# Weaving attention and channel work by hand on TensorE: a four-batch attention and ResMLP kernel

## The chip, the cores and the metric

The kernel runs on one core of a Trainium2 chip. The metric is the device time of one execution in microseconds (us); lower is better. The profile is one traced execution. Its engines are PE (TensorE, matmuls), PEld (its weight loads), DVE (VectorE), ACT (ScalarE), POOL (GpSimd) and SP (SyncE, which here only issues transfers).

## The reference

Shapes: batch 4, 8 heads, 768 positions, head width 64; then a block of width 512 with a hidden width of 2048.

```python
# P: 8 x 8 per head, five rounds of exp and row/column normalising of sort_net
k_sorted = einsum('bhij,bhjcd->bhicd', P, k_blocks)      # mixes blocks of 96 positions
v_sorted = einsum('bhij,bhjcd->bhicd', P, v_blocks)
scores = q_block @ k_sorted_block.T / 8                   # inside each block only
x = softmax(scores) @ v_sorted_block                      # -> (b, 768, 512)
u = x + lam * einsum('ts,bsd->btd', w_tok, alpha1 * x + beta1)
out = u + lam * (relu((alpha2 * u + beta2) @ w_ch1) @ w_ch2)
```

## The kernel before

Each batch does the same work on TensorE. I use the kernel's names: **v** and **k** mix the blocks of values and keys; **sc** (scores) and **x** (value products) are the attention; **tok** is the position mix, which needs all of x; **h** and **ch** are the two channel layers, in two halves (hf) of three tiles each. The work of one batch's attention runs beside the channel layers of the batch before. A small class wraps each engine; where its `fixed` is set, instructions keep the order in which the program names them, and elsewhere a scheduler orders them when the program is built.

```python
    class Engine:
        ...
                ins = getattr(self.eng, name)(*args, **kwargs)
                if self.fixed:
                    tc.keep_in_program_order(ins)

    def load_q(b):            # queries of batches 2, 3: six loads by GpSimd, one buffer
        ...
        qn = att.tile([128, NT, H, D], F16, name="qn", tag="qn", bufs=1)
        for kt in range(NT):
            pool.dma_start(qn[:, kt, :, :], q[b].rearrange("h (p kt) d -> kt p h d", kt=NT)[kt])

    def cross_q(b):           # ... and six transposes, issued by SyncE
        with tc.issue_after(regroup[b - 1].ins):
            for kt in range(NT):
                nc.sync.dma_start_transpose(
                    qT_of[b][:, :, kt, :], qn_of[b][:, kt, :, :].rearrange("p h d -> p (h d)")
                )

    def mix_v(b, banks=2, ...):
        ...                    # matmuls into PSUM, copies to vA, then through memory and back:
        nc.sync.dma_start(vscr[b, ...], vA[...])                       # x2
        regroup[b] = nc.sync.dma_start(Vs[b % NV][...], vscr[b]...)    # x2

    def emit_attention(b):
        ...
        prev = [emit_scores(b, 0, g) for g in range(2)]
        for h4 in range(1, H4):
            cur = [emit_scores(b, h4, g) for g in range(2)]
            emit_pv(b, h4 - 1, prev, x128, xs)       # value products; VectorE evicts them
            prev = cur
            if h4 == H4 - 1:
                gather(0, 384)                       # three small copies into x
        emit_pv(b, H4 - 1, prev, x128, xs)
        gather(384, C)

    def moe_ch(b, hf, kks=range(3)):
        for kk in kks:
            kt = 3 * hf + kk
            ...
            ost = att.tile([128, C], FT, name="ost", tag="ost", bufs=2)
            ...                # 16 matmuls into cps
                dve.tensor_tensor(cps[:], cps[:], lamB[:, lo:hi], ALU.mult)
                dve.tensor_tensor(ost[:, lo:hi], cps[:], u_of[b][kt][:, lo:hi], ALU.add)
                nc.sync.dma_start(out[b, kt * 96:(kt + 1) * 96, lo:hi], ost[0:96, lo:hi])
                ...            # and one more store of 32 rows

    # the main loop (TensorE, ScalarE, VectorE not fixed from here on)
    for b in range(1, B):
        if b > 1:
            if b > 2:
                cross_q(b)
            mixing_matrices(b)
            mix_v(b)
            ...
            mix_k(b)
        emit_attention(b)
        if b == 1:
            moe_ch(0, 0, (2,))
        else:
            moe_h(b - 1, 0)
            moe_ch(b - 1, 0)
        moe_h(b - 1, 1)
        moe_a(b)                                    # tok, and the transposes of u
        moe_ch(b - 1, 1)
        if b == 1:
            load_q(2)
            cross_q(2)
```

The softmax here doesn't subtract the row's maximum and nothing guards it: scores larger than these inputs give would overflow.

Of the kernel before, what the change touches and what calls it, by code (L numbers as in the profile page):

```python
# [7 lines left out]
FT = mybir.dt.float32  # L8
F16 = mybir.dt.float16
# [7 lines left out]
def kernel(  # L17
# [24 lines left out]
    BLK = S // NB  # L42
# [212 lines left out]
    def load_weights():  # L255
        for g in range(4):
            pool.dma_start(W1p[:, :, g * 512:(g + 1) * 512], w1v[:, :, g * 512:(g + 1) * 512])
        load_raw(1, 1)
        for g in range(4):
            pool.dma_start(W2p[:, g * 4:(g + 1) * 4, :], w2v[:, g * 4:(g + 1) * 4, :])  # L260

# [65 lines left out]
    def mix_v(b, banks=2, groups=range(6), copies=(act.copy, dve.tensor_copy, act.copy)):  # L327
        raw = raw_of[(b, 1)]
        lhsT = bigV[b][:].rearrange("p g i -> p (g i)")
        if b not in vA_of:  # L330
            vA_of[b] = att.tile([128, HB, D], F16, name="vA", tag="vA", bufs=1)
        vA = vA_of[b]
        for n in groups[::banks]:
            vps = (psb if banks == 1 else psa)([128, banks, 512], FT, "v_ps")
            for nn in range(banks):
                pe.matmul(vps[:, nn, :], lhsT, raw[:, (n + nn) * 512:(n + nn + 1) * 512], start=True, stop=True)
            copies[n // banks % len(copies)](
                vA[:, n * 8:(n + banks) * 8, :].rearrange("p t d -> p (t d)"), vps[:].rearrange("p n x -> p (n x)")
            )
        if groups[-1] < 5:  # L340
            return
        for th in range(2):
            nc.sync.dma_start(
                vscr[b, :, :, th * HB:(th + 1) * HB, :].rearrange("h i t d -> (h i) t d"),
                vA[th * 64:(th + 1) * 64, :, :],
            )
        for par in range(2):
            regroup[b] = nc.sync.dma_start(
                Vs[b % NV][par * HB:(par + 1) * HB, :, 0:D],
                vscr[b].rearrange("h i (tt par) d -> par tt (h i) d", par=2)[par],  # L350
            )

    def mix_k(b, share=(4, 0, 4), gs=range(3)):
        raw = raw_of[(b, 0)]
        rhs = bigP[b][:].rearrange("p g i -> p (g i)")
        if b not in kT_of:
            kT_of[b] = att.tile([128, H4 * NB, BLK], F16, name="kT", tag="kT", bufs=2)
        kv_ = kT_of[b][:].rearrange("p c (par th tp) -> p th c par tp", th=2, par=2)
        for g in gs:
            kps = psa([128, 8, 128], FT, "k_ps")  # L360
            for tp in range(8):
                t0 = (8 * g + tp) * 128
                pe.matmul(kps[:, tp, :], raw[:, t0:t0 + 128], rhs, start=True, stop=True)
            for par in range(2):
                for h2 in range(2):
                    src = kps[par * 64:(par + 1) * 64, :, h2 * 64:(h2 + 1) * 64].rearrange(
                        "p n (th c) -> p th c n", th=2
                    )
                    dst = kv_[h2 * 64:(h2 + 1) * 64, :, :, par, 8 * g:8 * g + 8]
                    if 2 * par + h2 < share[g]:  # L370
                        dve.tensor_copy(dst, src)
                    else:
                        act.copy(dst, src)
# [15 lines left out]

    def mix_k0(h4):  # L390
        if 0 not in kT_of:
            kT_of[0] = att.tile([128, H4 * NB, BLK], F16, name="kT", tag="kT", bufs=2)
        mix_heads(0, h4, kT_of[0][:, h4 * NB:(h4 + 1) * NB, :], (act.copy, dve.tensor_copy))

    vT0 = []
# [13 lines left out]

    x_of = {}  # L410

    def emit_scores(b, h4, g, spins=0):
        kT = kT_of[b]
        qT = qT_of[b]
        blocks = ((0, 1, 2, 6), (3, 4, 5, 7))[g] if b == 0 else range(4 * g, 4 * g + 4)
        sps = psa([128, 2, 4, 128], FT, "sc_ps")
        spin(sps[:, 0, :, :].rearrange("p i x -> p (i x)"), spins)
        for ii, i in enumerate(blocks):
            for h2 in range(2):
                rows = slice(h2 * 64, (h2 + 1) * 64)  # L420
                pe.matmul(
                    sps[0:BLK, h2, ii, 0:BLK], kT[rows, h4 * NB + i, :], qT[rows, h4, :, i * 16:(i + 1) * 16],
                    start=True, stop=True,
                )
        et = att.tile([BLK, 2, 4, BLK], F16, name="et", tag="et", bufs=4)
        act.activation(
            et[:].rearrange("p a i (r kt) -> p (a i) r kt", kt=NT),
            sps[0:BLK].rearrange("p a i x -> p (a i) x")[:, :, 0:BLK].rearrange("p n (kt r) -> p n r kt", kt=NT),
            AF.Exp, scale=scale,
        )  # L430
        return et
# [49 lines left out]
            xps[:, :, :, 0:D], recip[:].unsqueeze(3).to_broadcast([128, 2, 3, D]), ALU.mult,  # L481
        )

    def emit_attention(b):
        x128 = moep.tile([128, NT, C], F16, name="x128", tag="x128", bufs=2)
        xs = moep.tile([BLK, 2, C], F16, name="xs", tag="xs", bufs=1)
        x_of[b] = x128

        def gather(lo, hi):
            for a in range(3):  # L490
                dve.tensor_copy(x128[96:128, a:a + 4:3, lo:hi], xs[32 * a:32 * a + 32, :, lo:hi])

        prev = [emit_scores(b, 0, g) for g in range(2)]
        for h4 in range(1, H4):
            cur = [emit_scores(b, h4, g) for g in range(2)]
            emit_pv(b, h4 - 1, prev, x128, xs)
            prev = cur
            if h4 == H4 - 1:
                gather(0, 384)
        emit_pv(b, H4 - 1, prev, x128, xs)  # L500
        gather(384, C)


    w_tokT = const([128, NT, S], F16, "w_tokT")
    rs = const([128, NT], FT, "rs")
# [131 lines left out]

    def moe_h(b, hf, which=range(HT)):
        if (b, hf) not in hT_of:
            hTa = moep.tile([128, 12, 384], BF, name="hTa", tag="big", bufs=1)  # L640
            hTb = moep.tile([128, HT - 12, 384], BF, name="hTb", tag="hTb", bufs=1)
            hT_of[(b, hf)] = [hTa[:, m, :] if m < 12 else hTb[:, m - 12, :] for m in range(HT)]
        for m in which:
            hps = psb([128, 384], FT, "h_ps")
            for ci in range(CT):
                pe.matmul(
                    hps[:], W1p[:, ci, m * 128:(m + 1) * 128], a2T_of[b][hf][:, ci, :],
                    start=(ci == 0), stop=(ci == CT - 1),
                )
            act.activation(hT_of[(b, hf)][m], hps[:], AF.Relu)  # L650

    def moe_ch(b, hf, kks=range(3)):
        hT = hT_of[(b, hf)]
        for kk in kks:
# [3 lines left out]
            for lo, hi in ((0, 384), (384, C)) if last else ((0, C),):  # L658
                cps = psb([128, hi - lo], FT, "ch_ps")
                for m in range(HT):  # L660
                    pe.matmul(
                        cps[:], hT[m][:, kk * 128:(kk + 1) * 128], W2p[:, m, lo:hi],
                        start=(m == 0), stop=(m == HT - 1),
                    )
                dve.tensor_tensor(cps[:], cps[:], lamB[:, lo:hi], ALU.mult)
                dve.tensor_tensor(ost[:, lo:hi], cps[:], u_of[b][kt][:, lo:hi], ALU.add)
                nc.sync.dma_start(out[b, kt * 96:(kt + 1) * 96, lo:hi], ost[0:96, lo:hi])
                (nc.scalar if last else nc.sync).dma_start(
                    out[b, TAIL + kt * 32:TAIL + (kt + 1) * 32, lo:hi], ost[96:128, lo:hi]
                )  # L670


    ets = {}
# [51 lines left out]
    moe_row(range(2, NT))  # L725
    for kt in range(2, NT):
        moe_add(0, kt)
    load_raw(1, 0)
    load_q(1)
    for kt in range(2):  # L730
        dve.scalar_tensor_tensor(
            u_of[0][kt][:], b1lB[:], rs[:, kt:kt + 1], x_of[0][:, kt, :], op0=ALU.mult, op1=ALU.add
# [12 lines left out]
    stack = ExitStack()  # L745
    for eng in order:
        stack.enter_context(tc.issue_after(eng.ins))
    moe_h(0, 0, range(5))
    for n in range(6):
        moe_h(0, 0, range(5 + n, 6 + n))  # L750
        mix_v(1, 1, range(n, n + 1), (dve.tensor_copy,))
    pool.tensor_copy(gate[:], Vs[1][0:1, 0, 0:2])
    load_raw(2, 1)
    load_raw(2, 0)
    pool.fixed = False
    moe_h(0, 0, range(11, HT))
    moe_turn(0, 1)
    stack.close()
    pe.fixed = True
    for kk in range(2):  # L760
        moe_ch(0, 0, (kk,))
        mix_k(1, gs=((0, 1), (2,))[kk])
        for h4 in range(2 * kk, 2 * kk + 2):
            turn_q(1, h4, dve.tensor_copy)
    pe.fixed = False
    for b in range(1, B):
        if b > 1:
            if b > 2:
                cross_q(b)
            mixing_matrices(b)  # L770
            mix_v(b)
            if b == 2:
                opened = pool.tensor_copy(gate[:], Vs[0][0:1, 0, 0:2])
                with tc.issue_after(opened.ins):
                    load_q(3)
                    load_raw(3, 1)
                    load_raw(3, 0)
            mix_k(b)
        emit_attention(b)
        if b == 1:  # L780
            moe_ch(0, 0, (2,))
        else:
            moe_h(b - 1, 0)
            moe_ch(b - 1, 0)
        moe_h(b - 1, 1)
        moe_a(b)
        moe_ch(b - 1, 1)
        if b == 1:
            load_q(2)
            cross_q(2)  # L790
    for hf in range(2):
        moe_h(B - 1, hf)
        moe_ch(B - 1, hf)


# [28 lines left out]
```

## Time and profile before

| | before |
|---|---|
| median of 3 runs | 268.52 us (268.40 to 269.82) |
| profiled span | 266.8 us, full TensorE clock |
| TensorE busy | 257.6 us, 97% |
| batches 1, 2 and 3 (my cuts) | 60.8, 58.8, 58.8 us |

The lines themselves are in the prediction. "Busy" of TensorE is modelled and overlaps, so the prediction works with the distance from one matmul's start to the next.

### The profile page before, as it was taken

What the parts mean: (1) busy time and instruction counts of PE and PEld (TensorE: products, weight loads), DVE (VectorE), ACT (ScalarE), POOL (GpSimd) and SP (SyncE); (2) the same over time, 40 slices, a digit from 0 to 9 for tenths busy, and PEclk for the clock granted to TensorE, in tenths of its full rate; (3) what the DMA queues carried; (4) which work ended last, traced back from release to release, by engine and by line L of the source; (5) the groups of instructions that cost most, each with busy time, mean ns of one, the idle gap of its engine ahead of it and who ended that gap; (6) DMA issues with size and microseconds to landing.
All of it is one profiled execution on the core that took longest, in us unless ns stands there. A gap on an engine that the chain in (4) does not pass through costs nothing.

```text
span 266.8 us, 5149 instructions
## 1 busy us (share of the span) xinstructions
PE 257.6 (97%) x2049; PEld 141.6 (53%) x2059; DVE 154.8 (58%) x333; ACT 125.8 (47%) x232; POOL 92.5 (35%) x100
## 2 busy tenths in 40 slices
PE   7799999999999999999999999999999999999993
PEld 2467745565565444554565444554565445545542
DVE  5878788629567966722585966704675962042033
ACT  3376757643585312980375404970474305504600
POOL 8524689203575615007917225002409000000000
PEclk9999999999999999999999999999999999999999
DMA  6999999999999544499996342494200432012012
GB/s 83 174 208 251 207 210 207 211 216 112 211 157 155 113 84 117 114 82 89 202 211 136 61 100 80 118 98 62 80 2 2 81 76 79 2 39 79 2 39 79
DMA packets 62423, 30.88 MB, mean 116 GB/s; under 512 B 48888, under 2 KB 58112, under 8 KB 62400
## 3 DMA queue, kind: packets, MB, share of 16 engines
q0 software_dynamic: 23024, 15.60, 39.4%
q1 hardware_dynamic: 39280, 14.89, 32.6%
q8 instruction: 16, 0.26, 0.4%
q14 instruction: 7, 0.06, 0.1%
q10 hardware_dynamic: 96, 0.07, 0.1%
HBM read 32.78 MB, written 8.65 MB: 155 GB/s over the span
## 4 chain that ended last, share of the span: by engine, by line
PE 89%; ACT 4%; DVE 4%; issue 1%; DMA 1%; DVEq 0%; ACTq 0%
PE ch_ps L65 31%; PE h_ps L65 30%; PE tok_ps L65 12%; PE x_ps L65 5%; PE sc_ps L65 4%; ACT kT L65 2%; PE v_ps L65 2%; PE k_ps L65 1%; PE q_ps L65 1%; ACT et L65 1%; DVE csum L65 1%; DVE P L65 1%; PE m_ps L65 1%; DVE rsum L65 1%; DMA P<-in_sort_net_dram 1%
## 5 line engine op out<-in xcount | busy, mean ns | idle before, releaser
L65 PE MATMUL h_ps<-a2T,W1p 128*128 128x384 bf16 x512 | 93.4, 326 | 0.1
L65 ACT ACTIVATE hTa<-h_ps 128x384 bf16<-128x384 f32 x96 | 45.9, 492 | 68.1 <-PE h_ps L65 67.0
L65 PE MATMUL ch_ps<-W2p,hTa 128*128 128x512 bf16 (+2 forms) x290 | 65.9, 370 | 0.5
L65 PEld LDWEIGHTS <-W1p 128*128 128x128 bf16 x512 | 47.5, 98 | 30.3 <-issue 0.9
L65 DVE TENSOR_TENSOR ch_ps<-ch_ps,lamB 128x512 f32<-128x512 f32 (+2 forms) x25 | 16.9, 676 | 63.2 <-PE ch_ps L65 60.5
L65 POOL TENSOR_SCALAR u<-b1lB,rs 128x512 f32<-128x512 f32 x18 | 28.8, 1610 | 64.1 <-DVE ost L65 59.3
L65 PEld LDWEIGHTS <-hTa 128*128 128x128 bf16 x300 | 28.7, 98 | 32.4
L65 PE MATMUL tok_ps<-x,w_tokT 128*128 128x512 f16 x144 | 32.1, 379 | 0.0
L65 POOL TENSOR_TENSOR u<-x,u 128x512 f32<-128x512 f16 x22 | 25.3, 1181 | 18.1 <-DVE x L65 17.3
L65 ACT ACTIVATE et<-sc_ps 96x768 f16<-96x768 f32 x32 | 24.9, 807 | 11.7 <-PE sc_ps L65 11.7
L65 ACT CAST u<-u 128x512 f16<-128x512 f32 x24 | 14.8, 618 | 24.8 <-DVE u L65 24.8
L65 PE MATMUL ch_ps<-W2p,hTb 128*128 128x512 bf16 (+2 forms) x100 | 25.0, 371 | 0.0
L65 PEld LDWEIGHTS <-w_tokT 128*128 128x128 f16 x180 | 14.8, 97 | 16.1
L65 DVE TENSOR_TENSOR tok_ps<-tok_ps,a1lB 128x512 f32<-128x512 f32 x24 | 16.5, 692 | 7.3 <-PE tok_ps L65 7.3
L65 DVE CAST kT<-k_ps 64x512 f16<-64x512 f32 x24 | 16.5, 688 | 3.4 <-PE k_ps L65 3.0
L65 DVE TENSOR_TENSOR x<-x_ps,recip 96x512 f16<-96x512 f32 (+2 forms) x32 | 17.6, 554 | 0.9
L65 DVE TENSOR_TENSOR u<-tok_ps,u 128x512 f32<-128x512 f32 x24 | 16.4, 688 | 1.7
L65 ACT ACTIVATE hTb<-h_ps 128x384 bf16<-128x384 f32 x32 | 15.3, 497 | 3.8 <-PE h_ps L65 3.4
L65 DVE TENSOR_TENSOR ost<-ch_ps,u 128x512 f32<-128x512 f32 (+2 forms) x25 | 16.6, 665 | 0.6
L65 POOL DMA_DIRECT2D qn<-in_q_dram x18 | 15.5, 875 | 4.2 <-PE q_ps L65 3.4
L65 PEld LDWEIGHTS <-hTb 128*128 128x128 bf16 x100 | 9.6, 98 | 10.9
L65 PEld LDWEIGHTS <-et 96*128 96x128 f16 (+2 forms) x288 | 12.4, 99 | 4.6 <-issue 1.2
(95 smaller groups left out, 214.7 us busy)
## 6 DMA issues: line engine op xcount, KB each, us to landing
out_dram<-ost SPq DMA_DIRECT2D x23, 192.0 KB, 2.2
raw<-in_v_dram POOLq DMA_DIRECT2D x8, 384.0 KB, 8.9
raw<-in_k_dram POOLq DMA_DIRECT2D x8, 384.0 KB, 10.9
vscr<-vA SPq DMA_DIRECT2D x6, 384.0 KB, 4.4
Vs<-vscr SPq DMA_DIRECT2D x6, 384.0 KB, 7.7
W1p<-in_moe_w_ch_dram POOLq DMA_DIRECT2D x4, 512.0 KB, 10.1
W2p<-in_moe_w_ch_dram POOLq DMA_DIRECT2D x4, 512.0 KB, 17.9
qn<-in_q_dram POOLq DMA_DIRECT2D x12, 128.0 KB, 5.8
```

Source lines behind the costliest of these rows:

```text
L65: ins = getattr(self.eng, name)(*args, **kwargs)
```

## The change

Its intent is to spend channel matmuls as filler: whenever the attention would wait for an eviction, a counted number of h or ch matmuls stands in between. Both score groups of a head pair are issued together. Batch 1's key mixes and query transposes move into the first channel layer. W2 is loaded later, batch 1's keys and queries earlier. In batch 1's attention, five output tiles (ch(0,0) and two tiles of ch(0,1)) are now computed where the h work of the second half stood.

```diff
+        load_raw(1, 0)            # in load_weights, ahead of W2
+        load_q(1)
+    def load_w2():                # called later, where these two loads were
...
-            kT_of[b] = att.tile([...], name="kT", tag="kT", bufs=2)
+            kT_of[b] = att.tile([...], name="kT", tag="kT", bufs=1)
...
+    def emit_pair(b, h4):
+        pair = [psa([128, 2, 4, 128], FT, "sc_ps") for _ in range(2)]
+        for g in range(2):
+            score(b, h4, range(4 * g, 4 * g + 4), pair[g])
+        return [emit_exp(ps) for ps in pair]
...
+        yield 0, lambda: scores(0)          # attention_steps: (us of filler ahead, step)
+        yield 2.4, lambda: scores(1)
+        yield first, lambda: values(0)
+        yield 2.2, lambda: scores(2)
+        yield 2.4, lambda: values(1)
+        yield 2.2, lambda: scores(3)
+        yield 2.4, lambda: values(2)
+        yield 2.4, lambda: values(3)        # values(2), values(3) also gather into x
...
-            hTa = moep.tile([128, 12, 384], BF, name="hTa", tag="big", bufs=1)
-            hTb = moep.tile([128, HT - 12, 384], BF, name="hTb", tag="hTb", bufs=1)
+            hT = moep.tile([128, HT, 384], BF, name="hT", tag=("big", "hT1")[hf], bufs=1)
...                                          # moe_h yields 0.65 per tile, moe_ch 0.216 per matmul
+    for n in range(3):                      # inside the first channel layer
+        mix_k(1, gs=(n,))
+        run(moe_h(0, 0, range(10 + 2 * n, 11 + 2 * n)))
+        turn_q(1, n, dve.tensor_copy)
+        run(moe_h(0, 0, range(11 + 2 * n, min(12 + 2 * n, HT))))
+    turn_q(1, 3, dve.tensor_copy)
...
     for b in range(1, B):
+        if b == 1:
+            fill = chain(moe_h(0, 1), moe_ch(0, 0), moe_ch(0, 1, (0, 1)))
+            steps = [(0.6, lambda: mixing_matrices(2)), (0.6, lambda: mixing_matrices(3)), (0.8, lambda: None)]
+        else:
+            fill = chain(moe_h(b - 1, 0), moe_ch(b - 1, 0), moe_h(b - 1, 1), moe_ch(b - 1, 1, (0,)))
+            steps = [...]                   # mixes of v and k, with 1.8 to 3.0 us between
+        weave(fill, steps + list(attention_steps(b, 5.6 if b == 1 else 5.3)))
+        run(fill)
         moe_a(b)
-        moe_ch(b - 1, 1)
+        run(moe_ch(b - 1, 1, (2,) if b == 1 else (1, 2)))
         if b == 1:
             load_q(2)
             cross_q(2)
```

More of the change, by code (lines that the diff above doesn't have):

```diff
@@ L332, in mix_v @@
         vA = vA_of[b]
-        for n in groups[::banks]:
+        for n in range(groups[0], groups[-1] + 1, banks):
             vps = (psb if banks == 1 else psa)([128, banks, 512], FT, "v_ps")
@@ L356, in mix_k @@
         if b not in kT_of:
-            kT_of[b] = att.tile([128, H4 * NB, BLK], F16, name="kT", tag="kT", bufs=2)
+            kT_of[b] = att.tile([128, H4 * NB, BLK], F16, name="kT", tag="kT", bufs=1)
         kv_ = kT_of[b][:].rearrange("p c (par th tp) -> p th c par tp", th=2, par=2)
@@ L391, in mix_k0 @@
         if 0 not in kT_of:
-            kT_of[0] = att.tile([128, H4 * NB, BLK], F16, name="kT", tag="kT", bufs=2)
+            kT_of[0] = att.tile([128, H4 * NB, BLK], F16, name="kT", tag="kT", bufs=1)
         mix_heads(0, h4, kT_of[0][:, h4 * NB:(h4 + 1) * NB, :], (act.copy, dve.tensor_copy))
@@ L410, with score @@
     x_of = {}
-    def emit_scores(b, h4, g, spins=0):
-        kT = kT_of[b]
-        qT = qT_of[b]
-        blocks = ((0, 1, 2, 6), (3, 4, 5, 7))[g] if b == 0 else range(4 * g, 4 * g + 4)
-        sps = psa([128, 2, 4, 128], FT, "sc_ps")
-        spin(sps[:, 0, :, :].rearrange("p i x -> p (i x)"), spins)
+    def score(b, h4, blocks, sps):
         for ii, i in enumerate(blocks):
@@ L421, in emit_scores, with emit_exp @@
                 pe.matmul(
-                    sps[0:BLK, h2, ii, 0:BLK], kT[rows, h4 * NB + i, :], qT[rows, h4, :, i * 16:(i + 1) * 16],
-                    start=True, stop=True,
-                )
+                    sps[0:BLK, h2, ii, 0:BLK], kT_of[b][rows, h4 * NB + i, :],
+                    qT_of[b][rows, h4, :, i * 16:(i + 1) * 16], start=True, stop=True,
+                )
+    def emit_pair(b, h4):
[3 more added lines that the diff above has]
+        return [emit_exp(ps) for ps in pair]
+    def emit_scores(b, h4, g, spins=0):
+        sps = psa([128, 2, 4, 128], FT, "sc_ps")
+        spin(sps[:, 0, :, :].rearrange("p i x -> p (i x)"), spins)
+        score(b, h4, ((0, 1, 2, 6), (3, 4, 5, 7))[g], sps)
+        return emit_exp(sps)
+    def emit_exp(sps):
         et = att.tile([BLK, 2, 4, BLK], F16, name="et", tag="et", bufs=4)
@@ L482, in pv_tiles, with attention_steps @@
         )
-    def emit_attention(b):
+    def attention_steps(b, first):
         x128 = moep.tile([128, NT, C], F16, name="x128", tag="x128", bufs=2)
@@ L487, in emit_attention, with scores, values, weave @@
         x_of[b] = x128
-        def gather(lo, hi):
-            for a in range(3):
-                dve.tensor_copy(x128[96:128, a:a + 4:3, lo:hi], xs[32 * a:32 * a + 32, :, lo:hi])
-        prev = [emit_scores(b, 0, g) for g in range(2)]
-        for h4 in range(1, H4):
-            cur = [emit_scores(b, h4, g) for g in range(2)]
-            emit_pv(b, h4 - 1, prev, x128, xs)
-            prev = cur
-            if h4 == H4 - 1:
-                gather(0, 384)
-        emit_pv(b, H4 - 1, prev, x128, xs)
-        gather(384, C)
+        ets = {}
+        def scores(h4):
+            ets[h4] = emit_pair(b, h4)
+        def values(h4):
+            emit_pv(b, h4, ets[h4], x128, xs)
+            if h4 > 1:
+                lo, hi = ((0, 384), (384, C))[h4 - 2]
+                for a in range(3):
+                    dve.tensor_copy(x128[96:128, a:a + 4:3, lo:hi], xs[32 * a:32 * a + 32, :, lo:hi])
+        yield 0, lambda: scores(0)
[6 more added lines that the diff above has]
+        yield 2.4, lambda: values(3)
+    def weave(fill, steps):
+        for gap, step in steps:
+            filled = 0
+            while filled < gap:
+                took = next(fill, None)
+                if took is None:
+                    break
+                filled += took
+            step()
     w_tokT = const([128, NT, S], F16, "w_tokT")
@@ L639, in moe_h @@
         if (b, hf) not in hT_of:
-            hTa = moep.tile([128, 12, 384], BF, name="hTa", tag="big", bufs=1)
-            hTb = moep.tile([128, HT - 12, 384], BF, name="hTb", tag="hTb", bufs=1)
-            hT_of[(b, hf)] = [hTa[:, m, :] if m < 12 else hTb[:, m - 12, :] for m in range(HT)]
+            hT = moep.tile([128, HT, 384], BF, name="hT", tag=("big", "hT1")[hf], bufs=1)
+            hT_of[(b, hf)] = [hT[:, m, :] for m in range(HT)]
         for m in which:
@@ L650, in moe_h @@
             act.activation(hT_of[(b, hf)][m], hps[:], AF.Relu)
+            yield 0.65
     def moe_ch(b, hf, kks=range(3)):
@@ L664, in moe_ch @@
                     )
+                    if m < HT - 1:
+                        yield 0.216
                 dve.tensor_tensor(cps[:], cps[:], lamB[:, lo:hi], ALU.mult)
@@ L670, in moe_ch, with run @@
                 )
+                yield 0.216
+    def run(units):
+        for _ in units:
+            pass
     ets = {}
@@ L727 @@
         moe_add(0, kt)
-    load_raw(1, 0)
-    load_q(1)
+    load_w2()
     for kt in range(2):
@@ L747 @@
         stack.enter_context(tc.issue_after(eng.ins))
-    moe_h(0, 0, range(5))
+    pe.fixed = True
+    run(moe_h(0, 0, range(3)))
     for n in range(6):
-        moe_h(0, 0, range(5 + n, 6 + n))
+        run(moe_h(0, 0, range(3 + n, 4 + n)))
         mix_v(1, 1, range(n, n + 1), (dve.tensor_copy,))
@@ L755 @@
     pool.fixed = False
-    moe_h(0, 0, range(11, HT))
+    run(moe_h(0, 0, range(9, 10)))
     moe_turn(0, 1)
+    for n in range(3):
[4 more added lines that the diff above has]
+    turn_q(1, 3, dve.tensor_copy)
     stack.close()
     pe.fixed = True
-    for kk in range(2):
-        moe_ch(0, 0, (kk,))
-        mix_k(1, gs=((0, 1), (2,))[kk])
-        for h4 in range(2 * kk, 2 * kk + 2):
-            turn_q(1, h4, dve.tensor_copy)
@@ L765, with chain, mixes @@
-    pe.fixed = False
+    def chain(*parts):
+        for part in parts:
+            yield from part
+    def mixes(b, n):
+        return lambda: mix_v(b, 2, range(2 * n, 2 * n + 2), ((act.copy, dve.tensor_copy, act.copy)[n],) * 3)
     for b in range(1, B):
-        if b > 1:
+        if b == 1:
+            fill = chain(moe_h(0, 1), moe_ch(0, 0), moe_ch(0, 1, (0, 1)))
+            steps = [(0.6, lambda: mixing_matrices(2)), (0.6, lambda: mixing_matrices(3)), (0.8, lambda: None)]
+        else:
@@ L768 @@
             if b > 2:
                 cross_q(b)
-            mixing_matrices(b)
-            mix_v(b)
-            if b == 2:
-                opened = pool.tensor_copy(gate[:], Vs[0][0:1, 0, 0:2])
-                with tc.issue_after(opened.ins):
-                    load_q(3)
-                    load_raw(3, 1)
-                    load_raw(3, 0)
-            mix_k(b)
-        emit_attention(b)
-        if b == 1:
-            moe_ch(0, 0, (2,))
-        else:
-            moe_h(b - 1, 0)
-            moe_ch(b - 1, 0)
@@ L785, with later @@
-        moe_h(b - 1, 1)
+            fill = chain(moe_h(b - 1, 0), moe_ch(b - 1, 0), moe_h(b - 1, 1), moe_ch(b - 1, 1, (0,)))
+            steps = [
+                (0.0, mixes(b, 0)), (0.0, mixes(b, 1)), (1.8, mixes(b, 2)),
+                (1.8, lambda: mix_k(b, gs=(0,))), (1.8, lambda: mix_k(b, gs=(1,))),
+                (2.4, lambda: mix_k(b, gs=(2,))), (3.0, lambda: None),
+            ]
+            if b == 2:
+                def later():
+                    opened = pool.tensor_copy(gate[:], Vs[0][0:1, 0, 0:2])
+                    with tc.issue_after(opened.ins):
+                        load_q(3)
+                        load_raw(3, 1)
+                        load_raw(3, 0)
+                steps.insert(3, (0.0, later))
@@ L791 @@
     for hf in range(2):
-        moe_h(B - 1, hf)
-        moe_ch(B - 1, hf)
+        run(moe_h(B - 1, hf))
+        run(moe_ch(B - 1, hf))
 _INS = ['q', 'k', 'v', 'sort_net', 'moe_alpha1', 'moe_beta1', 'moe_w_tok', 'moe_alpha2', 'moe_beta2', 'moe_w_ch1', 'moe_w_ch2', 'moe_lam']
```

## The prediction

> **What bounds the kernel now.** I read the page's busy table and its chain first, then a table of stretches, one per batch, then the TensorE timeline inside one stretch. The page:
>
> ```profile
> PE 257.6 (97%) x2049; PEld 141.6 (53%) x2059; DVE 154.8 (58%) x333; ACT 125.8 (47%) x232; POOL 92.5 (35%) x100
> ...
> PE 89%; ACT 4%; DVE 4%; issue 1%; DMA 1%; DVEq 0%; ACTq 0%
> ```
>
> TensorE is busy 97% of the span and is 89% of the chain that ended last. A busy figure of modelled, overlapping ends doesn't say how much is lost, so I cut the span at the points where one batch hands over to the next (my cuts: the first h_ps matmul of batch 0 at 42.7, the mixing-matrix matmul of batch 2 at 103.5, that of batch 3 at 162.3, and the end of batch 3's attention round at 221.1):
>
> ```profile
> 42.70:103.50 60.80, 60.55 (x476) 33.19 (x478) 42.24 (x82) 29.37 (x55) 26.19 (x28) 1.00 1.07 156
> 103.50:162.30 58.80, 58.49 (x419) 30.78 (x420) 35.10 (x71) 28.24 (x52) 24.58 (x24) 1.00 0.84 121
> 162.30:221.10 58.80, 58.49 (x420) 30.90 (x422) 35.10 (x71) 28.25 (x52) 14.19 (x11) 1.00 0.42 71
> 221.10:262.50 41.40, 41.30 (x238) 22.71 (x238) 8.94 (x14) 15.71 (x32) 0.00 (x0) 1.00 0.14 40
> ```
>
> The columns are the stretch, its length, then busy us of PE, PEld, DVE, ACT, POOL, the clock, DMA. The clock is full throughout. The first three stretches are what the change rewrites: 178.4 us. The last one and everything before 42.7 keep their order of work.
>
> Next, what a matmul really takes: the distance of one start to the next, from the timeline. In long runs this is 162 ns for h_ps, 216 for ch_ps, tok_ps and v_ps, 56 for k_ps and uT_ps. These are full-array matmuls (128 rows), and they follow each other without loss. The score matmuls, 64 rows each, do not:
>
> ```profile
> 115.39 0.33 PE L65 MATMUL h_ps<-a2T,W1p 128*128 128x384 bf16 x1
> 115.65 0.56 PE L65 MATMUL sc_ps<-qT,kT 64*96 64x96 f16 x15
> 116.14 0.66 PE L65 MATMUL h_ps<-a2T,W1p 128*128 128x384 bf16 x3
> 116.92 0.38 PE L65 MATMUL sc_ps<-qT,kT 64*96 64x96 f16 x8
> 117.23 0.50 PE L65 MATMUL h_ps<-a2T,W1p 128*128 128x384 bf16 x2
> 117.66 0.38 PE L65 MATMUL sc_ps<-qT,kT 64*96 64x96 f16 x8
> ```
>
> The single h at 115.39 is followed at 115.65: 0.256 us instead of 0.162, so 0.093 us on the way in. Eight scores then hold TensorE 0.31 us (116.92 to 117.23), but fifteen only 0.49 (115.65 to 116.14). So seven more scores cost 0.18, or 25 ns each, and a fixed part of about 0.11 is the way out. **A lone group of 8 costs 0.093 + 0.311 = 0.404; a group of 16 would cost about 0.093 + 0.512 = 0.605.**
>
> **What the Trainium skill says.** "TensorEngine Tiling (Array Packing)", Key Properties: "Changing tiling mode (not just tile) drains the TensorE". The trace agrees: loss appears only where 64-row scores or 64-column q transposes meet full-array work (q group, way in 0.093), not at h to v or h to k. "TensorE: Matmul & The Clock Gate", Part 3, says that matmuls keep strict order and only weight loads are pulled ahead; so a matmul that waits holds all behind it, and a fixed order moves where the waits fall. "SBUF — State Buffer", on the pair of ports that VectorE and GpSimd share, calls it an exclusive lock. The trace is consistent: the last of three small copies into x takes up to 1.11 us (shortest 0.22) while GpSimd's first add runs.
>
> **The change, part by part.**
>
> *Scores in pairs.* Both groups of a head pair are issued back to back: four blocks of 16 in place of eight of 8 per batch. 8 x 0.404 = 3.23 becomes 4 x 0.605 = 2.42: minus 0.81 per batch, three batches, all on the path.
>
> *Batches 2 and 3: the stretch summed.* Full-array work: h 128 x 0.1624 = 20.79, ch 96 x 0.216 = 20.73, tok 36 x 0.216 = 7.77, v 6 x 0.216 = 1.30, k 24 x 0.056 = 1.35; together 51.94. Before: plus scores 3.23, value products 8 blocks x 0.257 = 2.06, the mixing matmul and its two switches 0.23: 57.46. Measured 58.8, so 1.3 us are true waits. I find them in the unmerged timeline: two waits of 0.17 before k_ps, 0.22 before an h, 0.18 before v_ps, 0.19 before a score, two of 0.12 before value products. All are cases of an operand or PSUM pair not yet evicted. The weave puts 1.8 to 3.0 us of h or ch between them. I check one: k_ps g0 needs four VectorE copies of 0.69 = 2.8 us; its PSUM is wanted again after two fills, 1.95 + 2.6 us. Good. After: 51.94 + 2.42 + 2.05 = 56.41 without waits, a gain of 2.4.
>
> *The wait that the weave adds.* The fill of batch 2 is 16 h (0.65 each), 48 ch, 16 h, 16 ch (0.216 each). Walking the steps with their gaps, 10 ch = 2.16 us remain after the last value product; then comes tok, which reads all of x. Before, the last value product was at 138.24 and tok at 144.03, nearly 6 us later. VectorE needs from the first matmul of that last product: 0.45 until the first group is out, reciprocal 0.20, product 0.69, reciprocal 0.20, two products 0.83, three gather copies 1.61 with the port clash, starts included: 4.05 us (before, product at 139.44 to last copy at 142.67 is 3.23; plus 0.69 ahead of it is 3.9). TensorE reaches tok at 0.52 + 0.04 + 2.16 = 2.72. Rows 0 and 3 come with the first copy, so tok's first two matmuls may run; the third is due at 3.15 and must wait until 4.1. **Cost 0.95 us in each of batches 2 and 3.** I allow 0.25 more for what a fixed order catches elsewhere. 56.41 + 0.95 + 0.25 = 57.6, against 58.8: minus 1.2 each.
>
> *Batch 1.* Full-array work 52.6 (the above, plus 12 uT). Before: q in two blocks of (0.093 + 0.932), 2.05; scores 3.23; values 2.06: 59.9 of 60.8, waits 0.9. After: q in four blocks of 12, each 0.093 + 11 x 0.034 + 0.152 = 0.62, so 2.47 (worse by 0.42); scores 2.42; values 2.05; two mixing matmuls, 0.45, moved here from batches 2 and 3: 60.0. VectorE is the doubt: tok evictions 4.0, v copies 4.1, a2T 0.9, k copies 5.6, q copies 2.0, mixing 2.0 are 18.6 us, of the 19.4 from 42.3 until the first scores. I put waits at 0.5: 60.5, minus 0.3. Here 20 ch = 4.3 us remain after the last value product, so tok does not wait.
>
> *Loads.* W2 moves from 27.3 to about 42; its landing took up to 18.7 us, so about 61 to 64, and its first use moves from 55.2 to about 70 because h(0,1) now precedes it: hidden. Keys and queries of batch 1 take W2's place at 27 to 32; GpSimd issued each once an earlier transfer had landed, at 29.09 and 31.60, and those are unchanged, so the affine preparation still ends near 34.9. No effect. The k buffer halves to one, reused two thirds of a batch after its last reader; the second hidden buffer only lets h(.,1) start before ch(.,0) ends. Neither frees a wait that I see now.
>
> **Sum:** 0.3 + 1.2 + 1.2 = 2.7. 268.5 - 2.7 = 265.8 us.
>
> **Rivals.** (a) *The waits vanish but tok takes all back*: if tok waits for the whole of x rather than its third row block, or VectorE evicts a ch_ps (1.4 us) ahead of the gather, the added wait is 1.4 to 2.7 per batch and the gain falls to 1 or to nothing: 267 to 269. For it: VectorE follows its own order. Against: GpSimd began its first add at 141.43, before the last copy at 142.67, so dependences are by region. (b) *VectorE becomes the bound in batch 1's first layer*, with k, q and v copies packed there: each microsecond late moves everything; 267 to 270. For: 18.6 of 19.4. (c) *No waits at all*: 2.4 + 2.4 + 0.8 = 5.6, 262.9. Against: the count of 2.16 against 4.05. (d) *The values' round trip through memory* meets W2 in the queues: Vs landed at 66.8 before; first use is now about 71.8, 5 us of room; a loss only if W2 delays it more.
>
> **Range and chances.** The floor without waits is 262.9, just past the 2% mark of 263.2, so faster needs nearly every wait gone: 0.04. Slower by over 2% means 273.9, 5.4 us lost in a schedule meant to remove 3: 0.03. Eight in ten: 264.0 to 268.6, the upper end being (a) or (b).
>
> **What would show it.** Right: score blocks of 16 holding 0.51 us; no waits ahead of k_ps; the stretches of batches 2 and 3 near 57.6; a gap of about 1 us in the first tok_ps matmuls of batches 2 and 3 but not of batch 1, with VectorE's x copies as releaser; TensorE's order up to 42 unchanged. Wrong: a tok gap near 0 or above 2, waits on k_ps or q_ps evictions between 45 and 62, or a wait on Vs or W2.

## More of the kernel before

The output tile `ost` matters later: there are two, VectorE writes one per output tile, and SyncE stores it with two transfers.

In SyncE's queue, from 59 to 90 us, one transpose of batch 2's queries goes out, then the last two stores of the first channel half, and only then the other five. The next output tile is due near 98, so nothing waits behind the transposes. The same answer held a warning one batch later:

```profile
128.79 12.89 SPq L149 DMA_TRANSPOSE qT<-qn  x5
141.77 0.53 SPq L667 DMA_DIRECT2D out_dram<-ost  x1
```

Five transposes hold the queue for 12.9 us, and an output tile that VectorE wrote by 132.7 is sent only at 141.8. Nothing waited for it there, since VectorE wrote the next tile only at 156.3.

One more view of the kernel before is needed for what follows. It is the timeline of SyncE's queue, from 59 to 90 us (start, duration, issuing line, transfer, how many):

```profile
59.21 2.46 SPq L348 DMA_DIRECT2D Vs<-vscr  x2
...
71.46 1.37 SPq L149 DMA_TRANSPOSE qT<-qn  x1
74.34 0.32 SPq L667 DMA_DIRECT2D out_dram<-ost  x1
74.71 0.46 SPq L668 DMA_DIRECT2D out_dram<-ost  x1
83.10 7.17 SPq L149 DMA_TRANSPOSE qT<-qn  x5
```

## The result, and the profile after

The changed kernel took **276.50 us** (median of 4, 274.51 to 277.31) against 268.54 for the kernel before in the same rounds. The ratio is 1.0274, with a 95% interval of 1.0205 to 1.0344: slower, where 265.8 had been predicted. (A ratio here is the mean time of one kernel's fast runs over that of the other's in the same rounds, so not quite the ratio of the medians.)

The page of the changed kernel: engines, the granted clock in 40 slices, and the chain that ended last.

```profile
PE 255.2 (94%) x2044; PEld 142.4 (52%) x2059; DVE 154.7 (57%) x333; ACT 124.9 (46%) x232; POOL 91.7 (34%) x100
...
PEclk9999999999999689999999999999999999999999
...
PE 76%; DVE 7%; DMA 6%; SPq 6%; ACT 2%; issue 1%; POOL 1%; DVEq 0%; ACTq 0%
```

TensorE's share of the chain fell from 89% to 76%. Transfers (DMA) and SyncE's queue (SPq), which had next to no part in it, now have 6% each. And the clock, full before, dips once. The stretches of batches 1 to 3 (columns as in the prediction; the stretch after them is as before, 41.50 us against 41.40). A batch is now cut at its first v matmul and no longer at its mixing matmul, since those of batches 2 and 3 (0.23 us each in the prediction's sum) moved into batch 1:

```profile
42.70:112.25 69.55, 61.93 (x477) 33.73 (x481) 41.89 (x86) 28.38 (x54) 28.07 (x28) 0.95 1.17 138
112.25:169.55 57.30, 56.38 (x416) 30.85 (x418) 35.13 (x68) 28.46 (x53) 23.49 (x23) 1.00 0.87 123
169.55:226.90 57.35, 56.43 (x416) 30.91 (x419) 34.79 (x68) 28.16 (x52) 13.29 (x11) 1.00 0.43 72
```

Batches 2 and 3 gained 1.5 us each (1.2 predicted; 57.3 us against 57.6). All the loss is in batch 1: 69.55 us in place of 60.8. The list of waits says for what (who waited for whom: us in total, times, longest):

```profile
DVE ost L65 <- DMA out_dram<-ost: 6.5, 1, 6.5
...
PE x_ps L65 <- DVE x L65: 5.6, 1, 5.6
...
PE tok_ps L65 <- DVE x L65: 1.4, 2, 0.7
...
PE x_ps L65 <- DMA Vs<-vscr: 1.3, 1, 1.3
```

The third line is the wait that had been predicted. The others are new. Read the first two as one chain: VectorE could not write an output tile, since the store that still read it had not landed; the eviction of the value products stood behind it in VectorE's order; so TensorE had no PSUM for the next ones. VectorE's timeline shows it (the reciprocal that the eviction needs is done at 86.33, but the eviction runs only after the output tile):

```profile
86.14 0.19 DVE L65 RECIPROCAL recip<-x_ps 96x8 f32<-96x8 f32 x1
92.84 0.69 DVE L65 TENSOR_TENSOR ost<-ch_ps,u 128x512 f32<-128x512 f32 x1 [6.50 <-DMA out_dram<-ost]
93.44 0.68 DVE L65 TENSOR_TENSOR x<-x_ps,recip 96x512 f16<-96x512 f32 x1
```

and TensorE's:

```profile
85.78 2.76 PE L65 MATMUL ch_ps<-W2p,hT 128*128 128x512 bf16 x12
94.18 0.65 PE L65 MATMUL x_ps<-Vs,et 96*128 96x65 f16 x8 [5.65 <-DVE x L65]
```

Why had the store not landed? SyncE's queue, in the same view as before:

```profile
59.26 2.42 SPq L352 DMA_DIRECT2D Vs<-vscr  x2
66.96 21.63 SPq L149 DMA_TRANSPOSE qT<-qn  x6
88.68 0.53 SPq L700 DMA_DIRECT2D out_dram<-ost  x1
89.26 1.25 SPq L701 DMA_DIRECT2D out_dram<-ost  x1
```

All six query transposes now stand ahead of the first store, and they hold the queue for 21.6 us. The first four go out as their query loads land, up to 73.1; the fourth alone then takes 11.4 us to issue. The output tile ready at 78.9 waits until 88.7 to be sent. Before, in the same queue, no store was due behind batch 2's transposes.

The pause costs more than itself. After 5.65 us without work TensorE comes back at half clock. Two stretches right after it (the clock is the number after the last bracket):

```profile
94.00:95.90 1.90, 1.29 (x16) 1.11 (x18) 1.80 (x7) 0.00 (x0) 1.26 (x1) 0.50 0.47 138
95.90:98.10 2.20, 2.15 (x6) 0.85 (x6) 2.14 (x7) 0.00 (x0) 0.00 (x0) 0.54 0.00 0
```

In the second stretch ch matmuls start 427 ns apart instead of 216. The Trainium skill, "TensorE: Matmul & The Clock Gate", Part 1, says that idling for about a 3.4 us window halves the clock until the array has been busy for as long. By the clock records in the trace it fell at 91.08, about 2.6 us after TensorE had run out of work, and was full again at 97.91, 3.7 us after the work resumed. So the way back fits the page; the way down came sooner, and sooner still in the sixth experiment below.

From single starts I add up batch 1's losses on TensorE: 5.81 at that product, 0.48 at its second group (PSUM not yet evicted), about 1.0 at five ch matmuls at the low clock and 0.45 just ahead of them, and 1.49 at the first value product, which waited for Vs: 9.2 us. (The 0.45 is no wait that the trace shows: 19 of the 20 ch matmuls due here are recorded, and the missing one at half speed would fill it.) Batch 1 would have been near 60.3 without these losses; the prediction had 60.5.

The profiled run is the fastest of the four, 274.51 us. Where the other runs, up to 2.8 us longer, lost the rest was not traced.

### The profile page after: what moved, and what is told of

Same layout as the page of the kernel before. It is cut to its first block, busy times and chain, and to the rows that moved or that the text cites. A ratio compares the mean times of both kernels' runs of the same rounds, so it can differ in the third digit from the quotient of the medians.

```text
span 272.7 us, 5138 instructions
## 1 busy us (share of the span) xinstructions
PE 255.2 (94%) x2044; PEld 142.4 (52%) x2059; DVE 154.7 (57%) x333; ACT 124.9 (46%) x232; POOL 91.7 (34%) x100
## 4 chain that ended last, share of the span: by engine, by line
PE 76%; DVE 7%; DMA 6%; SPq 6%; ACT 2%; issue 1%; POOL 1%; DVEq 0%; ACTq 0%
PE h_ps L65 27%; PE ch_ps L65 24%; PE tok_ps L65 11%; SPq L149 6%; DMA qn<-in_q_dram 4%; PE x_ps L65 3%; PE sc_ps L65 3%; DVE x L65 2%; PE k_ps L65 1%; PE v_ps L65 1%; PE q_ps L65 1%; DMA out_dram<-ost 1%; POOL qn L65 1%; DVE csum L65 1%; DVE P L65 1%
## 5 line engine op out<-in xcount | busy, mean ns | idle before, releaser
L65 PE MATMUL h_ps<-a2T,W1p 128*128 128x384 bf16 x512 | 89.9, 326 | 0.0
L65 PE MATMUL ch_ps<-W2p,hT 128*128 128x512 bf16 (+2 forms) x385 | 86.8, 373 | 0.9 <-issue 0.2
L65 ACT ACTIVATE hT<-h_ps 128x384 bf16<-128x384 f32 x128 | 60.0, 492 | 47.4 <-PE h_ps L65 47.0
L65 PEld LDWEIGHTS <-W1p 128*128 128x128 bf16 x512 | 48.6, 98 | 32.2 <-issue 0.3
L65 PEld LDWEIGHTS <-hT 128*128 128x128 bf16 x400 | 38.0, 99 | 41.8 <-issue 1.6
L65 POOL TENSOR_SCALAR u<-b1lB,rs 128x512 f32<-128x512 f32 x18 | 28.2, 1576 | 55.2 <-DVE ost L65 55.2
L65 DVE RECIPROCAL recip<-x_ps 96x8 f32<-96x8 f32 (+1 forms) x32 | 6.2, 195 | 31.7 <-PE x_ps L65 31.4
L65 PE MATMUL x_ps<-Vs,et 96*128 96x65 f16 (+2 forms) x288 | 13.8, 197 | 7.2 <-DVE x L65 5.6
L65 DVE TENSOR_SCALAR a2T<-a2T,ab2col 128x384 bf16<-128x384 f16 x24 | 7.5, 376 | 5.6 <-DMA a2T<-u 5.0
```

## The experiments

Theory **Q**: the six transposes ahead of the stores in SyncE's queue cause the 5.8 us and what follows it. Rival **F**: the hand-made order starves TensorE, because VectorE is nearly full in batch 1 (this is rival (b) of the prediction). Rival **C**: the low clock is the cause and not a result. For the wait on Vs, theory **Q2** blames batch 2's query loads and rival **W** the late W2. The first, second and sixth experiments change the changed kernel; the third builds on the second, the fourth on the third, the fifth and the last on the fourth. All kernels gave correct results; each was timed beside the kernel before on its chip (269.25 us in the first four, 269.19 in the last three).

### Three output tiles

```diff
-            ost = att.tile([128, C], FT, name="ost", tag="ost", bufs=2)
+            ost = att.tile([128, C], FT, name="ost", tag="ost", bufs=3)
```

(and one buffer in place of two for the small `sel` tile, for room; two VectorE instructions on it change places, TensorE's order stays)

> The changed kernel with three output tiles (ost) in place of two; to make room, the small sel tile has one buffer instead of two. Theory Q (the six transposes of batch 2's queries sit ahead of the output stores in SyncE's queue; the stores keep the two ost tiles; VectorE, in order, waits 6.5 us for one; TensorE waits 5.8 us at a value product): VectorE's wait for out_dram<-ost goes from 6.5 to under 1, TensorE's 5.8 and the two smaller waits after it (0.48, 0.45) and the five half-speed matmuls (1.0) go: about 7.3 us less, 267.2 in the run of 274.5, while SyncE's transposes still take about 21 us and the wait of 1.5 for Vs stays. Rival F (the fixed order on TensorE itself starves, VectorE being the bound of batch 1): no change, 274 to 277. Rival C (the lowered clock is the cause and the wait its result): wait goes only in part, over 271.

Measured: **266.61 us** (4 runs, 265.16 to 266.92), ratio to before 0.9865 (0.9787 to 0.9942). VectorE's wait for out_dram<-ost is gone from the list of waits, TensorE's 5.8 and the two after it too, and the clock of batch 1 is 1.00. SyncE still spends 67.2 to 84.7 on the transposes. Batch 1 takes 61.90 us, 7.7 less. So a spare tile is enough to break the chain, with the transposes where they were: Q's second half, the tile, stands. F and C fall, for neither the order on TensorE nor anything about the clock was touched; in the changed kernel, too, the clock fell only after the pause had begun.

### The stores first

```diff
-        with tc.issue_after(regroup[b - 1].ins):
+        with tc.issue_after((stores[(0, 2)] if b == 2 else regroup[b - 1]).ins):
```

(`stores` keeps each output tile's second store. Compared instruction by instruction, only SyncE's order differs from the changed kernel.)

> The changed kernel with the transposes of batch 2's queries held, on SyncE alone, behind the third output store; every other engine has the same instructions in the same order. Theory Q: the same as three ost tiles, about 267.2, with VectorE's wait for out_dram<-ost under 1 us and no gap over 0.5 at the fourth value product of batch 1; the wait for Vs (1.5) and those before tok in batches 2 and 3 (0.87 each) stay. Rival F: no change, 274 to 277.

Measured: **266.86 us** (4 runs, one of them slow; fast ones 266.08 to 267.08), ratio 0.9882 (0.9808 to 0.9957). SyncE's queue:

```profile
78.75 0.33 SPq L702 DMA_DIRECT2D out_dram<-ost  x1
79.12 1.07 SPq L703 DMA_DIRECT2D out_dram<-ost  x1
...
87.73 7.84 SPq L151 DMA_TRANSPOSE qT<-qn  x6
```

The stores go out when their tiles are ready, and the same six transposes, begun at 87.7, hold the queue for 7.8 us instead of 21.6. The second remedy gives the same time as the first. That is the cause pinned from both ends of the chain: the queue's order, and the tile that it kept.

### The query loads held until Vs has landed

```diff
-    pool.tensor_copy(gate[:], Vs[1][0:1, 0, 0:2])
+    opened1 = pool.tensor_copy(gate[:], Vs[1][0:1, 0, 0:2])
...
-            load_q(2)
+            with tc.issue_after(opened1.ins):
+                load_q(2)
```

> As e2_stores_first, and the loads of batch 2's queries held on GpSimd behind the copy that shows that Vs has landed. Theory Q2 (those six loads, issued at 59.7, share the queues with the second half of Vs<-vscr, issued at 59.6, which lands at 73.0 instead of 68.4): Vs lands by 69, the 1.5 us wait at the first value product of batch 1 goes, about 265.7. Rival W (the late load of W2 slows the round trip; its last piece lands at 59.9): Vs still lands at about 73, no change against e2_stores_first.

Measured: **265.67 us** (265.50 to 266.01), ratio 0.9849 (0.9788 to 0.9910). The second transfer Vs<-vscr, issued at 59.5, landed at 68.1 instead of 72.8 in the second experiment, and the wait at the first value product is gone, with W2 as late as in the changed kernel. Q2 stands, W falls. (The same edit lets the loads of raw keys and values go out ahead of the query loads, at 65.6, so only the query loads left that place.) What moved the query loads is worth seeing: they need the one `qn` buffer, which batch 1's last query transpose frees. The change put those transposes into the first channel layer, so the loads could start at 59.7; in the kernel before, the first started at 65.9 and the other five from 76.3.

### More filler left ahead of tok

```diff
-        weave(fill, steps + list(attention_steps(b, 5.6 if b == 1 else 5.3)))
+        weave(fill, steps + list(attention_steps(b, 5.6 if b == 1 else 3.6)))
```

> As e3_q2_hold, with 3.6 instead of 5.3 us of fill ahead of the first value product of batches 2 and 3, so that 1.7 us more of ch work is left after the last. Theory T (tok waits for the last gather copy): the gap of 0.87 us in tok_ps of both batches goes to nothing, 1.7 us less than e3_q2_hold, about 264.0. Rival: the first value product now waits for exp or PSUM and the gain is given back: no change.

Measured: **264.02 us** (263.88 to 264.48), ratio 0.9790 (0.9729 to 0.9850). TensorE's timeline at tok in batch 2 of the changed kernel:

```profile
151.33 0.68 PE L65 MATMUL x_ps<-Vs,et 96*128 96x65 f16 x16
151.84 2.33 PE L65 MATMUL ch_ps<-W2p,hT 128*128 128x512 bf16 x10
154.00 0.59 PE L65 MATMUL tok_ps<-x,w_tokT 128*128 128x512 f16 x2
155.31 2.97 PE L65 MATMUL tok_ps<-x,w_tokT 128*128 128x512 f16 x13 [0.71 <-DVE x L65]
```

Ten ch matmuls, two of tok, then the wait, as the prediction counted it (the third start is 0.87 us late, 0.95 predicted). With the new filler there is none: 15 recorded ch matmuls, then tok without a break. From first matmul to first matmul, batches 2 and 3 take 56.67 and 56.43 us, where the prediction's sum without waits was 56.41.

### The pairs undone

```diff
-        yield 0, lambda: scores(0)
-        yield 2.4, lambda: scores(1)
+        yield 0, lambda: scores(0, 0)
+        yield 0.6, lambda: scores(0, 1)
+        yield 1.8, lambda: scores(1, 0)
+        yield 0.6, lambda: scores(1, 1)
...                                          # likewise for the others
```

> As e4_tail with the score pairs undone: in each of the 12 pairs of batches 1 to 3 at least 0.6 us of h or ch work goes between the two groups and 0.6 less after them, so everything else keeps its place. Theory P (each switch between 64-row scores and full-array work costs about 0.2 us, way in and out): 12 x 0.20 = 2.4 us more than e4_tail, about 266.4. Rival (the pairing itself is worth nothing, the gain over the kernel before came from the waits only): the same as e4_tail, 264.0.

Measured: **266.94 us** (6 runs, 266.63 to 267.55), ratio to before 0.9915 (0.9894 to 0.9937). The stretches of batches 1 to 3, of the kernel with pairs (the fourth experiment; cut at round figures, so up to 0.1 us off the lengths above):

```profile
42.70:103.20 60.50, 60.21 (x477) 33.18 (x481) 40.92 (x83) 28.41 (x54) 28.16 (x28) 1.00 1.04 156
103.20:159.80 56.60, 56.15 (x414) 30.84 (x418) 35.94 (x71) 28.65 (x53) 23.43 (x23) 1.00 0.89 126
159.80:216.30 56.50, 56.13 (x415) 30.86 (x419) 34.91 (x69) 28.61 (x52) 13.31 (x11) 1.00 0.43 74
```

and of the kernel without:

```profile
42.90:104.35 61.45, 61.43 (x482) 33.11 (x480) 40.85 (x83) 28.83 (x54) 28.24 (x28) 1.00 1.03 153
104.35:161.95 57.60, 57.53 (x419) 30.83 (x418) 35.96 (x71) 28.96 (x53) 23.35 (x23) 1.00 0.89 124
161.95:219.30 57.35, 57.35 (x419) 30.84 (x418) 34.86 (x69) 28.93 (x52) 13.46 (x11) 1.00 0.43 72
```

Each batch is about 0.9 us longer, 2.8 us in all or 0.23 per pair; 2.4 was expected. The price of a switch between 64-row scores and full-array work is real. That it is above the 0.203 us per pair of the prediction is explained by the trace: a group of 16 scores holds TensorE for 0.491 us and not 0.512, so a pair saves 0.224.

### The large loads held instead

In the changed kernel, with its SyncE order kept, the loads of batch 2's raw keys and values are held on GpSimd behind the first value product:

```diff
-    load_raw(2, 1)
-    load_raw(2, 0)
...
+                opened = pool.tensor_copy(gate[:], x_of[1][0:1, 0, 0:2])
+                with tc.issue_after(opened.ins):
+                    load_raw(2, 1)
+                    load_raw(2, 0)
```

> The changed kernel, its order on SyncE kept (six query transposes ahead of the stores), but the four loads of batch 2's raw keys and values held on GpSimd until the first value product of batch 1 is in x, about 74. Theory R (the transposes crawl because those loads, issued at 67 to 69, fill the queues before them: five of six land only after the last load, 88.6): the transposes now end by about 78, the stores get through, VectorE's wait for out_dram<-ost under 1.5 us, time about 267; the 1.5 wait for Vs stays. Rival (the transposes are slow in themselves or wait only for the query loads): SyncE still held for about 20 us and 274 to 277.

Measured: **270.58 us** (6 runs, 269.23 to 272.10), ratio to before 1.0050 (1.0018 to 1.0081). Half a hit, half a miss. SyncE's queue:

```profile
67.03 9.99 SPq L149 DMA_TRANSPOSE qT<-qn  x6
79.29 0.33 SPq L700 DMA_DIRECT2D out_dram<-ost  x1
```

The transposes now take 10 us, so in the changed kernel it was those loads, issued at 67.1 to 68.8 and landing 16 to 20 us later, that held them up. The single packets in the changed kernel's trace show how: from 76 to 82 us, 221 packets of GpSimd's queue (the loads) and 223 of SyncE's (the transposes) moved, one for one, but most of the loads' had 6144 bytes and almost all of the transposes' 256, so the loads moved 1,068 KB and the transposes 55. But the time was to be 267. The loads, now issued at 75.9, were in flight when the stores went out, and the store of 79.29 landed at 88.4, 9.1 us later; the usual for such a store is 2.2. VectorE waited 2.2 us for its tile, TensorE 1.5 at a value product and 0.6 at its second group, and the clock dropped again, for 3.4 us:

```profile
90.19 0.43 PE L65 MATMUL x_ps<-Vs,et 96*128 96x65 f16 x8 [1.32 <-DVE x L65]
91.09 0.43 PE L65 MATMUL x_ps<-Vs,et 96*128 96x65 f16 x8 [0.47 <-DVE xs L65]
...
91.40:94.80 3.40, 3.40 (x13) 1.20 (x11) 3.25 (x11) 0.00 (x0) 0.00 (x0) 0.50 0.01 2
```

So two waits of 1.5 and 0.6 us were enough to halve the clock, without a pause of 3.4 us. Freeing the queue is not enough: a store that shares the transfer engines with 1.5 MB of loads (four of 384 KB) is late as well, and two output tiles do not bridge that. In the runs above the third tile did, and so did transposes out of the way.

### The best version

As the fourth experiment, with batch 1's query transposes in two blocks of 24 and the two mixing matmuls side by side, for fewer switches:

```diff
-        turn_q(1, n, dve.tensor_copy)
+        if n > 0:
+            for h4 in range(2 * n - 2, 2 * n):
+                turn_q(1, h4, dve.tensor_copy)
...
-            steps = [(0.6, lambda: mixing_matrices(2)), (0.6, lambda: mixing_matrices(3)), (0.8, lambda: None)]
+            steps = [(0.6, lambda: mixing_matrices(2)), (0.0, lambda: mixing_matrices(3)), (1.8, lambda: None)]
```

> As e4_tail, with the four query transposes of batch 1 on TensorE in two blocks of 24 instead of three entries of 12, 12 and 24 split by one h unit, and the mixing matmuls of batches 2 and 3 one after the other. By the switch costs (way in 0.093 and way out 0.122 for q, about 0.19 for the mixing matmul): two q switches and one mixing switch fewer, minus 0.6 us, about 263.4. Rival: VectorE's copies of q come later together and the first scores of batch 1 wait: 264.0 or more.

Measured: **263.35 us** (6 runs, 262.75 to 265.06), ratio 0.9789 (0.9758 to 0.9821). Batch 1 takes 59.57 us in its profile, 0.9 less than in the fourth experiment. Over the whole time the two kernels' intervals against the kernel before overlap almost entirely (0.9790 and 0.9789), so the runs do not show that this last step is a gain. Both versions beat the kernel before by about 2.1% (the intervals reach from 1.5 to 2.7% and from 1.8 to 2.4%) and, by medians taken on different chips, the changed one by more than 12 us.

## Why the prediction was wrong, and where it was right

**Switch costs and the sums: right, with two sizes off.** Batches of 57.3 us where 57.6 was predicted, the gap of 0.87 us in tok's third matmul in batches 2 and 3 and none in batch 1, and the floor of 56.41 that the fourth experiment reaches at 56.43. The third experiment, which takes away only the two waits that were not foreseen, gives 265.67 us; 265.8 was predicted. Its batch 1 takes 60.49 us; 60.5 was predicted. That last agreement is partly luck: the prediction had 60.0 of work and 0.5 of waits, but the trace shows one wait of 0.18, while each of the four q blocks took 0.69 us and not 0.62. The other size: 16 scores held TensorE for 0.49 us and not 0.51. The line read for it had 15 scores, at 25 ns each; single starts show them in twos every 45 ns, so the sixteenth adds next to nothing.

**Batch 1: the term that failed.** The step is "I put waits at 0.5: 60.5, minus 0.3". Batch 1 measured 69.55, or 9.1 more: 1.49 at the wait on Vs and 7.7 from the wait for an output tile. The prediction's waits were counted on TensorE and VectorE, through operands and PSUM. The two output tiles and the queue that empties them were not counted. Five output tiles had moved into the time when batch 2's loads and query transposes run; the part headed "Loads" looked only at whether a load comes in time for its reader, and ended with "No effect".

**Rival (d): right in kind, with a wrong room.** It said that Vs would be late only if W2 slowed it, with 5 us to spare. The 66.8 came from GpSimd's check, which reads the first of two transfers; the second landed at 68.4, so the room was 3.4 us. And it was batch 2's query loads, not W2, that took it away (the third experiment). A wait on Vs was on the prediction's list of signs of being wrong, and it came.

**Rival (b), VectorE as the bound of the first layer: wrong.** From 42.7 to 71 TensorE shows no wait over 0.2 us. Later VectorE did make TensorE wait, but it was itself idle for 6.5 us at the time.

**The range** had 268.6 as its upper end and put "slower by over 2%" at 0.03, on the ground that 5.4 us would have to be lost. One wait that was off every list lost 7.7 of the 9.2, a quarter of it by the lowered clock and the restart (1.0, 0.48, 0.45). The first experiment, which takes it away, shortens batch 1 by the same 7.7.

What stays open: why the wait of the fourth transpose is 11.4 us in one run and 8.1 in another, and with it why the changed kernel's runs spread over 2.8 us, where those of the third and fourth experiments spread over 0.6. The trace gives each packet's queue, but not which transfer it belongs to. Why waits of 1.5 and 0.6 us halved the clock in the sixth experiment, when one of 1.5 us at the first value product of the same run did not, is open too.

## What to carry to other kernels

When work moves in time, move its outputs too: for each output tile ask which queue sends it, what stands ahead of it in that queue at the new time, and how many tiles there are to wait in. An order that is kept passes a late store on to everything behind it, here from SyncE to VectorE to TensorE, so a third tile or an explicit order in the queue, about 10 us by medians taken on different chips, was worth more here than the new order on the bounding engine. And a sum of start-to-start distances by kind, with the price of each switch, predicted the stretches without new waits to 0.3 us, partly by errors that cancel; what it needs beside it is a list of every buffer in the stretch, the ones on the way out included.

## What the Trainium skill lacked or had wrong

- "TensorEngine Tiling (Array Packing)", Key Properties, says that a change of tiling mode drains TensorE and gives no figure. Here entering 64-row scores from full-array work cost 0.093 us and leaving them about 0.1; undoing 12 pairs cost 2.8 us, 0.23 each.
- "DMA: Bandwidth & Descriptors", Queues, rings and completion order, says that a transfer engine goes round the queues that have work, packet by packet. The packets of the changed kernel agree: 221 against 223 from 76 to 82 us. It does not say how late a transfer of small packets gets: 55 KB moved there against 1,068, a store of 192 KB beside 1.5 MB of loads landed after 9.1 us instead of 2.2, and six transposes that take SyncE 7.8 us took it 21.6.
- No page that I read says that a transpose in SyncE's queue can hold the stores behind it for so long; one held it for 11.4 us by itself.
- "TensorE: Matmul & The Clock Gate", Part 1, has the half clock come after at least one idle window of about 3.4 us. The measurements differ: in the changed kernel the clock fell about 2.6 us into a pause, and in the sixth experiment it was 0.50 for 3.4 us after waits of 1.5 and 0.6 us with 8 matmuls between them. The half speed itself is as the page says: ch matmuls started 427 ns apart instead of 216.
